# A quarter of the gate weights loaded early, on few partitions, in a decode kernel that streams a KV cache

## The chip, the cores and the metric

The kernel runs on one core of one Trainium2 chip. The metric is the device time of one execution in microseconds (us); the median of three runs before is 663.46 us.

## The reference, cut to what matters

```python
mod = (_silu(c) @ w_mod).reshape(c.shape[0], 6, 1, -1)     # c: 4 x 512, w_mod: 512 x 3072
sa, ca, ga, sb, cb, gb = (mod[:, 0].copy(), ..., mod[:, 5].copy())
h = _layernorm(x, axis=-1) * (1 + ca) + sa
x = x + ga * _A_ref(h, A_k_cache, A_v_cache, A_wq, A_wo)   # 4 tokens, 32 heads, 4096 cached keys, 128 per head
h = _layernorm(x, axis=-1) * (1 + cb) + sb
x = x + gb * _B_ref(h, B_w_in, B_w_sp, B_b_sp, B_w_out)    # gated MLP, 512 -> 1792 -> 512
return x
```

Everything is bf16. Attention reads two caches of 4 x 32 x 4096 x 128, 128 MiB each. The six sections of `w_mod` (512 columns each) make shifts, scales and gates; the last section gives `gb`, which multiplies the MLP's result just before the output. So `gb` is needed at the very end, though it depends on `c` and `w_mod` alone.

## The kernel before, in words

The kernel streams K and V once through three big buffers in SBUF: bA and bB hold K (64 KB on each of 128 partitions), bC holds V. Work goes in 32 rounds `i`, each for four heads of one batch; two rounds share a load of 8 MB (`load_k`, `load_v`, both issued on SP's queue at L145). In a round, DVE multiplies K by the query in two halves (`mult`, L376), PE adds up most of the products with identity matmuls (`reduce_d`, L384) and DVE the rest (L396, L407). After every second round DVE finds the maximum, ACT takes the exponentials into the tile pbd (L450), and PE multiplies them with V (`pv`, L505). A V load may start when `pv` has read the V before it; a K load when DVE has summed the K before it. The order is written out by hand in the loop over `i`, with no scheduler; each engine runs its instructions in the order in which the program names them.

Before the rounds, bC holds wq in its first 32 KB per partition, five of the six sections of w_mod behind it (`wm_sb`, one transfer, L127), and small tiles (`pre`). PE multiplies silu(c), laid out as columns in cT, with these sections (`mod_rows`, L272): the results stand as rows in `mrows` and are turned into columns by transposes (`mod_turn`, L282). Two sections are needed for the queries (L321, L329). The other three go through `late_mod_b`, called in round 0 between DVE's second multiplication and its first sum, which copies them into modT (L352). As soon as PE has read what lies in bC, the first V load replaces it.

At the end the last V load comes in four cuts (`TAIL`, 64, 32, 16 and 16 columns of 128), and bC is filled by `load_end`: the last part of wo in two transfers, w_in in two, w_out in two, and the gate section of w_mod in four (L596, `KG`), one for each quarter of its 512 rows, 128 partitions by 1 KB. The MLP's two products are `gate` (L825) and the one into `y` (L851); then comes the product of the gate section with cT (L859, 16 matmuls of 4 columns), DVE's chain that joins y, the layer norm's numbers and gb (L879 to L891), a transpose (L893), the residual (L895) and the output (L896).

A transfer adds to one of eight semaphores, which are given out in turn, four of ACT's transfers included. Before a transfer is issued, the eighth before it must have landed. In the kernel before there are 52 transfers on SP's queue and four on ACT's (c, x, and two single elements).

`ps_sm` gives out three small PSUM buffers in turn. `across` is an f32 product of a 128 x 128 matrix with a narrow tile (L216).

Of the kernel before, what the change touches and what calls it, by code (L numbers as in the profile page):

```python
# [8 lines left out]
BF16 = mybir.dt.bfloat16  # L9
F32 = mybir.dt.float32  # L10
# [6 lines left out]
HP = 8  # L17
# [1 line left out]
RD = 8  # L19
TAIL = (64, 32, 16, 16)  # L20
KIN = (slice(0, 2), slice(2, 4))
KG = tuple(slice(k, k + 1) for k in range(4))
JW = (slice(0, 4), slice(4, 7))
RW = (slice(0, 4), slice(4, 8))

# [26 lines left out]
def kernel(  # L52
# [16 lines left out]
    nc = tc.nc  # L69
    P = 128  # L70
    B, _, D = A_x.shape
# [3 lines left out]
    DJ = D // P  # L75
# [4 lines left out]
    R = P // HQ  # L80
    G = 4
    NT = B * H // HQ
    GP = H // HP - 1
# [12 lines left out]
    ident_bf = front.tile([P, P], BF16, name="ident_bf")  # L96
# [3 lines left out]
    bufA, bufB, bufC = bufs  # L100
    consts = ctx.enter_context(tc.tile_pool(name="consts", bufs=1))
    wk = ctx.enter_context(tc.tile_pool(name="work", bufs=2))
    psum = ctx.enter_context(tc.tile_pool(name="psum", bufs=1, space=PSUM))
    KB = 1024
# [4 lines left out]
    def ps_sm(shape, dtype=F32):  # L109
        return psum.tile(shape, dtype, name="sm", bufs=3)  # L110

    def ps_q():
        return psum.tile([P, 512], F32, name="qps", bufs=1)

    wq_sb = Arena(bufC, 0, 32 * KB).tile([P, DJ, H * DH], BF16)
    wm_sb = Arena(bufC, 32 * KB, 52 * KB).tile([P, DJ, 5 * D], BF16)
    pre = Arena(bufC, 52 * KB, 64 * KB)
    cx_sb = pre.tile([2 * B, D], BF16, name="cx_sb")
# [5 lines left out]
    nc.scalar.preload_act_table_set("natural_log_exp_and_others")  # L124
    nc.sync.dma_start(out=wq_sb, in_=A_wq.rearrange("(p j) n -> p j n", p=P))
    wm = w_mod.rearrange("(p j) n -> p j n", p=P)
    nc.sync.dma_start(out=wm_sb, in_=wm[:, :, 0:5 * D])  # L127

    def kv_view(cache, i):
        if i < N0:  # L130
# [17 lines left out]
    def load_k(i):  # L148
        if i < N0:
            load(bufs[i // 2 % 2], kv_view(A_k_cache, i), (NJ, NJ) if i == 0 else (NP,))  # L150
        else:
            load(kts[i], kv_view(A_k_cache, i), (NJ,))
# [5 lines left out]
            load(vts[i], kv_view(A_v_cache, i), TAIL if i == L else (NJ,))  # L158

    load_k(0)  # L160
    load_k(2)

    make_identity(nc, ident_bf)
    ident_f = consts.tile([P, P], F32, name="ident_f")
# [16 lines left out]
    def spread(n, pattern, axis, **sizes):  # L181
# [18 lines left out]
        out=far, in0=half, scalar1=-1.0, scalar2=-NEG, op0=ALU.add, op1=ALU.mult  # L200
    )
    nc.gpsimd.tensor_scalar(
        out=fars, in0=far[:, :, None].to_broadcast([P, 2, R // 2]), scalar1=-1.0, scalar2=None, op0=ALU.mult
    )
    cT = consts.tile([P, DJ, B], BF16, name="cT")
    pbd8 = consts.tile([P, NP, HP], BF16, name="pbd")
    nc.gpsimd.memset(pbd8, 0.0)
    pbds = pbd8.rearrange("p n q -> p (n q)").rearrange("p (k n q) -> p k n q", k=4, q=HQ)
# [42 lines left out]
    for j in range(DJ):  # L251
        nc.tensor.transpose(cxp[:, j, :], cx_sb[:, j:D:DJ], ident_bf[0:2 * B, 0:2 * B])
    cps, xps = cxp[:, :, 0:B], cxp[:, :, B:2 * B]
    cx = pre.tile([P, DJ, B], F32, name="cx")
    nc.vector.tensor_copy(out=cx, in_=cps)
    sg = pre.tile([P, DJ, B], F32, name="sg")
    nc.vector.tensor_scalar(
        out=sg, in0=cx, scalar1=-60.0, scalar2=-1.0, op0=ALU.max, op1=ALU.mult
    )
# [5 lines left out]
    mrows = pre.tile([P, D], F32, name="mrows")  # L265
# [13 lines left out]
    def mod_turn(n):  # L279
        mps = ps_sm([P, DJ, n * R])  # L280
        for j in range(DJ):
            nc.tensor.transpose(mps[:, j, :], mrows[0:n * R, j:D:DJ], ident_f[0:n * R, 0:n * R])  # L282
        return mps.rearrange("p j (s r) -> p s j r", s=n)[:, :, :, 0:B]
# [10 lines left out]
        out=hs, in0=modA[:, 1], scalar=1.0, in1=xn, op0=ALU.add, op1=ALU.mult  # L294
# [19 lines left out]
    def queries(n):  # L314
        h, b = divmod(n, B)
        gs = slice(h * GQ, (h + 1) * GQ)
        if b == 0:
            qr = ps_sm([P, GQ, DH])
            for k in range(DJ):
                for q in range(HQ):  # L320
                    nc.tensor.matmul(  # L321
                        qr[R * q:R * (q + 1)], lhsT=hT[:, k, :], rhs=wq_v[:, k, gs, q, :],
                        start=(k == 0), stop=(k == DJ - 1), tile_position=(0, R * q),
                    )
            nc.scalar.copy(out=qrow[:, h], in_=qr)
        qp = ps_q().rearrange("p (g d) -> p g d", g=GQ)
        npair = 1 if h and b == BL else 2
        for k in range(2):
            nc.tensor.matmul(  # L329
                qp[:, 0:npair], lhsT=eb2[k][:, b].rearrange("p k q r -> p (k q r)"),  # L330
                rhs=qrow[:, h, k:2 * npair:2], start=(k == 0), stop=(k == 1),
            )
        if npair == 1:
            nc.tensor.matmul(
                qp[:, 2:4], lhsT=eb[:, b].rearrange("p q r -> p (q r)"), rhs=qrow[:, h, 2:4],
                start=True, stop=True,
            )
            nc.scalar.copy(out=qbo, in_=qp[:, 2:4])
        nc.scalar.copy(out=qbp[:, 2 * h:2 * h + npair, b, :], in_=qp[:, 0:npair])  # L339

    for n in range(2 * B):
        queries(n)

    modT = consts.tile([P, 3 * DJ, B], F32, name="modT")
    g8 = consts.tile([P, 2, B], F32, name="g8")
    spf = consts.tile([P, 2], F32, name="spf")

    def late_mod_b():
        mps = mod_turn(3)
        sps = ps_sm([P, 2])  # L350
        nc.tensor.matmul(sps, lhsT=ones_b, rhs=sp_t, start=True, stop=True)
        nc.vector.tensor_copy(  # L352
            out=modT.rearrange("p (s j) b -> p s j b", s=3),
            in_=mps,
        )
        nc.vector.tensor_copy(out=spf, in_=sps)
        nc.gpsimd.tensor_copy(out=g8[:, 1, :], in_=spf[:, 0:1].to_broadcast([P, B]))
        cbT = modT[:, 2 * DJ:3 * DJ, :]
        nc.gpsimd.tensor_scalar_add(out=cbT, in0=cbT, scalar1=1.0)
# [208 lines left out]
    wo_sb = Arena(bufA, 0, 24 * KB).tile([P, GP * HP, D], BF16)  # L568
# [1 line left out]
    wol_sb = Arena(bufC, 0, 8 * KB).tile([P, HP, D], BF16)  # L570
    win_sb = Arena(bufC, 8 * KB, 22 * KB).tile([P, DJ, F], BF16)
    wout_sb = Arena(bufC, 22 * KB, 29 * KB).tile([P, NH, D], BF16)
    wg_sb = Arena(bufC, 29 * KB, 33 * KB).tile([P, DJ, D], BF16)
    tl = Arena(bufC, 33 * KB, 64 * KB)
    NL = GP * HP * DH

    def load_wo():
        nc.sync.dma_start(
            out=wo_sb.rearrange("p (k r) n -> p k r n", r=HP),
            in_=A_wo[0:NL].rearrange("(k p r) n -> p k r n", k=GP, p=P),  # L580
        )

    def load_end():
        wol = A_wo[NL:H * DH].rearrange("(p r) n -> p r n", p=P)
        for rs in RW:
            nc.sync.dma_start(out=wol_sb[:, rs], in_=wol[:, rs])
        win = B_w_in.rearrange("(p j) n -> p j n", p=P)
        for ks in KIN:
            nc.sync.dma_start(out=win_sb[:, ks], in_=win[:, ks])
        for js in JW:  # L590
            nc.sync.dma_start(
                out=wout_sb[:, js],
                in_=B_w_out[js.start * P:js.stop * P].rearrange("(p j) n -> p j n", p=P),
            )
        for ks in KG:
            nc.sync.dma_start(out=wg_sb[:, ks], in_=wm[:, ks, 5 * D:])  # L596

    acc = late.tile([P, DJ, B], F32, name="acc")
    st2 = late.tile([P, 2, B, DJ + 1], F32, name="st2")
# [73 lines left out]
    for i in range(NT):  # L673
        mult(i, 0)
        if i >= 1:
            scores(i - 1)
        for k in normed_in(i - 1):
            norm_b(k)
        pick = i - 3 if i % 2 == 0 and i >= 4 else None
        if i % 2 and 3 <= i < L:  # L680
            pv(i - 2)
        if i % 2 and i < N0:
            load_v(i)
        reduce_d(i, 0)
        if pick:
            o_pick(pick)
            o_cols(pick)
        if i == L:
            deal(2)
            pv(N0 - 1)  # L690
            load_end()
            nc.gpsimd.memset(pbd8, 0.0)  # L692
            nc.vector.memset(opss[1], 0.0)
            exps(N0)
        mult(i, 1)
        if i == 0:
            late_mod_b()
        for k in normed_in(i):
            norm_r(k)
        if pick:  # L700
            o_scale(pick)
        sum8(i, 0)
        if i == L:
            dealt(0, 0, 2 * B)
            dealt(2)
            o_pick(N0 - 1)
            nc.vector.memset(opss[0], 0.0)
        reduce_d(i, 1)
        sum_rest(i)
        for k in normed_in(i):  # L710
            norm_a(k)
        if i == L - 1:
            deal(0, 0, 2 * B)
        if i == L:
            o_cols(N0 - 1)
            project()
        if i % 2 and i + 3 < N0:
            load_k(i + 3)
        elif i == N0 - 3:
            load_k(N0)  # L720
            load_k(L)
        elif i == N0 - 1:
            load_wo()
            load_v(N0)
            late_consts()
        elif i == N0:
            load_v(L)
# [16 lines left out]
    for i in (N0, L):  # L744
        norm_a(i)
    nc.vector.tensor_reduce(
        out=sel32, in_=ident_f.rearrange("p (q r) -> p r q", r=R), axis=AX.X, op=ALU.add
# [69 lines left out]
    def gate(h, part):  # L817
# [26 lines left out]
        out=zz.rearrange("p f g b -> p g b f"), in0=z1[:, None].to_broadcast([P, 2, B, NH]),  # L844
        in1=st3[:, 0:2], op=ALU.mult,
    )
    y = ps_q()[:, 0:DJ * 2 * B].rearrange("p (j g b) -> p j g b", j=DJ, g=2)
    for js in JW:
        for j in range(DJ):
# [3 lines left out]
                    start=(j == 0 and f == 0), stop=(f == NH - 1), skip_group_check=True,  # L853
                )

    gb = ps_sm([P, DJ, B])
    for k in range(DJ):
        for j in range(DJ):
            nc.tensor.matmul(  # L859
                gb[:, j, :], lhsT=wg_sb[:, k, j * P:(j + 1) * P], rhs=cT[:, k, :],  # L860
                start=(k == 0 and j == 0), stop=(k == DJ - 1), skip_group_check=True,
            )
    mq3 = tl.tile([P, 2, B], F32, name="mq3")
    nc.vector.tensor_reduce(
# [62 lines left out]
```

## Time and profile before

| | |
|---|---|
| Median of 3 runs | 663.46 us (663.36 to 663.65) |
| Profiled execution: time, span | 663.69 us, 661.8 us |
| Moved by DMA | 283.07 MB, mean 428 GB/s |
| Queue of SP | 8016 packets, 282.73 MB, 99.0% of 16 engines' span |
| Busy: DVE, PE, ACT | 574.8, 309.7, 171.9 us |
| Largest waits of SP's queue | V landings 279.0 us, DVE's sums L396 180.1 us, PE's L505 86.1 us |
| Chain that ended last | DMA 64%, DVE 16%, PE 14%, ACT 4% |

The span runs from the first instruction to the last; 1.9 us of the execution's time lie outside it. Idle time of an engine that is not the bottleneck costs nothing. SP's queue is not an engine that moves data: it only issues transfers, and waits in it matter when the DMA engines run out of packets. Times in the text are from the span's start.

### The profile page before, as it was taken

To read this page: it belongs to the slowest core of one execution; us is meant where nothing else is said; L and a number is where in the kernel's file an instruction comes from. 1 tells how busy PE (TensorE), PEld (TensorE's weight loads), DVE (VectorE), ACT (ScalarE), POOL (GpSimd) and SP (SyncE) were. 2 spreads that over 40 slices of the span, in tenths; PEclk is the share of its full clock that TensorE was granted. 3 is DMA by queue.
4 is the path that set the end of the run, shared out by engine and by line. 5 is a ranking of instruction groups with operands and counts; after the bars stand their busy time and mean duration, and the time that the engine had idled before them with its cause. 6 is when DMAs were issued, how large, how long until landed. Compare 5 with 4: busy or idle time off the path is not lost.

```text
span 661.8 us, 5002 instructions
## 1 busy us (share of the span) xinstructions
PE 309.7 (47%) x2036; PEld 130.4 (20%) x2036; DVE 574.8 (87%) x367; ACT 171.9 (26%) x284; POOL 19.0 (3%) x56
## 2 busy tenths in 40 slices
PE   0554454536253463615336361534635245463885
PEld 0121121212021121202112120211212012121434
DVE  2269999999898998989899898979979898999943
ACT  1220414223060603206060330605023060503322
POOL 3000000000000000000000000000000000040100
PEclk9996686867677785767777576777756778675975
DMA  8999999999999999999999999999999999999997
GB/s 364 450 423 444 444 437 440 444 400 437 436 444 433 440 417 432 445 424 440 437 440 420 440 433 424 436 445 444 413 444 429 432 440 433 428 420 449 412 419 283
DMA packets 8060, 283.07 MB, mean 428 GB/s; under 512 B 860, under 2 KB 1380, under 8 KB 2916
## 3 DMA queue, kind: packets, MB, share of 16 engines
q1 hardware_dynamic: 8016, 282.73, 99.0%
q8 instruction: 16, 0.26, 0.1%
q14 instruction: 8, 0.07, 0.0%
q10 hardware_dynamic: 20, 0.01, 0.0%
HBM read 282.73 MB, written 0.00 MB: 427 GB/s over the span
## 4 chain that ended last, share of the span: by engine, by line
DMA 64%; DVE 16%; PE 14%; ACT 4%; issue 1%; SPq 0%; POOL 0%; ACTq 0%; DVEq 0%
DMA bC<-in_A_v_cache_dram 50%; PE ops L505 9%; DVE S L396 6%; DMA bA<-in_A_k_cache_dram 6%; DVE bA L376 4%; DMA bC<-in_A_wo_dram 4%; DMA bC<-in_w_mod_dram 4%; DVE bB L376 3%; ACT pbd L450 3%; PE red L384 3%; DVE S L407 1%; PE qps L329 1%; PE sm L321 1%; PE sm L272 1%; ACT qbp L339 0%
## 5 line engine op out<-in xcount | busy, mean ns | idle before, releaser
L450 ACT ACTIVATE pbd<-S,nb 32x256 bf16<-32x256 f32 x120 | 154.2, 1519 | 423.1 <-DVE nb L437 421.9
L376 DVE TENSOR_TENSOR bA<-bA,qbp 128x8192 bf16<-128x8192 bf16 x32 | 142.7, 4462 | 21.1 <-DMA bA<-in_A_k_cache_dram 21.1
L384 PE MATMUL red<-bB,ident_bf 128*128 128x512 bf16 x344 | 97.2, 441 | 116.2 <-DVE bB L376 116.0
L384 PE MATMUL red<-bA,ident_bf 128*128 128x512 bf16 x320 | 91.8, 446 | 121.0 <-DVE bA L376 121.0
L384 PEld LDWEIGHTS <-ident_bf 128*128 128x128 bf16 x664 | 72.0, 110 | 350.7 <-issue 195.0
L376 DVE TENSOR_TENSOR bB<-bB,qbp 128x8192 bf16<-128x8192 bf16 x28 | 123.7, 4417 | 14.1 <-DMA bB<-in_A_k_cache_dram 14.1
L505 PE MATMUL ops<-bC,pbd 128*32 128x512 bf16 x960 | 80.1, 507 | 67.3 <-DMA bC<-in_A_v_cache_dram 58.5
L396 DVE TENSOR_REDUCE S<-bA 128x48 f32<-128x6144 bf16 x16 | 104.7, 6542 | 0.0
L396 DVE TENSOR_REDUCE S<-bB 128x48 f32<-128x6144 bf16 x14 | 91.6, 6542 | 0.0
L505 PEld LDWEIGHTS <-pbd 128*32 128x32 bf16 (+1 forms) x1016 | 36.0, 122 | 117.4 <-issue 59.1
L450 ACT ACTIVATION_READ_ACCUMULATOR pbd<-S,nb 32x1 f32 x120 | 58.7, 489 | 0.0
L407 DVE TENSOR_REDUCE S<-red 128x64 f32<-128x512 f32 x64 | 43.7, 682 | 2.7 <-PE red L384 2.5
L464 POOL TENSOR_TENSOR rsb<-maskd,rs 128x8 f32<-128x8 f32 x15 | 3.1, 204 | 562.0 <-ACT pbd L450 562.0
L376 DVE TENSOR_TENSOR bB<-bB,qbo 128x8192 bf16<-128x8192 bf16 x4 | 17.6, 4411 | 0.0
L517 DVE TENSOR_REDUCE osb<-ops 128x128 f32<-128x512 f32 x17 | 11.8, 692 | 0.6
L514 DVE TENSOR_TENSOR ops<-ops,m 128x512 f32<-128x512 f32 x15 | 10.4, 693 | 0.0
L483 PE MATMUL sm<-rsb,inv_d 128*128 128x32 f32 (+2 forms) x12 | 2.9, 338 | 13.9 <-POOL rsb L464 13.9
L293 DVE SCALAR_TENSOR_TENSOR bC<-sm,bC 128x16 f32<-128x16 f32 x1 | 0.2, 175 | 10.1 <-PE sm L282 10.1
L450 ACT ACTIVATE pbd<-S,nM 32x128 bf16<-32x128 f32 x8 | 4.6, 576 | 11.6 <-POOL pbd L692 10.1
L420 DVE TENSOR_REDUCE mrow<-S 128x1 f32<-128x256 f32 (+1 forms) x17 | 6.9, 404 | 0.6
L272 PE MATMUL sm<-bC,cT 128*4 128x512 bf16 x20 | 3.7, 621 | 7.1 <-DMA bC<-in_w_mod_dram 7.1
L329 PE MATMUL qps<-bC 128*128 128x256 bf16 (+1 forms) x16 | 4.5, 382 | 4.1 <-ACT qbp L339 2.8
(159 smaller groups left out, 128.1 us busy)
## 6 DMA issues: line engine op xcount, KB each, us to landing
bA<-in_A_k_cache_dram SPq DMA_DIRECT2D x2, 4096.0 KB, 31.3
bB<-in_A_k_cache_dram SPq DMA_DIRECT2D x2, 4096.0 KB, 41.1
bC<-in_A_wq_dram SPq DMA_DIRECT2D x1, 4096.0 KB, 12.3
bA<-in_A_v_cache_dram SPq DMA_DIRECT2D x1, 4096.0 KB
bA<-in_A_wo_dram SPq DMA_DIRECT2D x1, 3072.0 KB, 39.9
bC<-in_w_mod_dram SPq DMA_DIRECT2D x1, 2560.0 KB, 17.9
bB<-in_A_v_cache_dram SPq DMA_DIRECT2D x1, 2048.0 KB, 31.9
bC<-in_B_w_in_dram SPq DMA_DIRECT2D x2, 896.0 KB, 24.1
```

What stands on the lines that cost most here:

```text
L272: nc.tensor.matmul(mp[R * s:R * s + B], lhsT=cT[:, k, :], rhs=wm_sb[:, k, (s0 + s) * D:(s0 + s + 1) * D], start=(k == 0), stop=(k == DJ - ...
L321: nc.tensor.matmul(qr[R * q:R * (q + 1)], lhsT=hT[:, k, :], rhs=wq_v[:, k, gs, q, :], start=(k == 0), stop=(k == DJ - 1), tile_position=(0 ...
L329: nc.tensor.matmul(qp[:, 0:npair], lhsT=eb2[k][:, b].rearrange("p k q r -> p (k q r)"), rhs=qrow[:, h, k:2 * npair:2], start=(k == 0), sto ...
L376: nc.vector.tensor_tensor(out=kt, in0=kt, in1=bc(q, KC), op=ALU.mult)
L384: nc.tensor.matmul(red, lhsT=ident_bf, rhs=kt[:, :, m * rd:(m + 1) * rd], start=(m == 0), stop=(m == DH // rd - 1),)
L396: nc.vector.tensor_reduce(out=st[i, "S"][:, n0:NJ], in_=kts[i][:, n0:NJ, :], axis=AX.X, op=ALU.add)
L407: nc.vector.tensor_reduce(out=st[i, "S"][:, kc * KC:kc * KC + on_pe(i, kc)], in_=st.pop((i, "red", kc)), axis=AX.X, op=ALU.add,)
L420: nc.vector.tensor_reduce(out=mrow, in_=S, axis=AX.X, op=ALU.max)
L450: nc.scalar.activation(out=pbd8[r, :, 2 * q + h] if pair(i) else pbds[r, i % 4, :, q], in_=S[r, :], func=AF.Exp, bias=nM[r, h:h + 1], scal ...
L505: nc.tensor.matmul(ops_of(i)[g:g + rows], lhsT=pb[:, n, :], rhs=vt[:, n, :], start=(m < 4), stop=(m >= end - 4), tile_position=(0, g),)
L514: nc.vector.tensor_tensor(out=ops, in0=ops, in1=sel[:, :, None].to_broadcast([P, G, DH]), op=ALU.mult)
L517: nc.vector.tensor_reduce(out=osb, in_=ops.rearrange("p g d -> p d g"), axis=AX.X, op=ALU.add)
```

## The change

128 of the 512 rows of the gate section go into bC early, in place of wq, and are multiplied with silu(c) in round 0. The result is a fourth group of rows in `mrows`, turned together with the other three, and kept in modT. The remaining 384 rows are loaded at the end as before, three to a partition.

- The 128 rows: 120 as 12 partitions of 10 rows, by four transfers of three partitions each (0, 4, 8; then 1, 5, 9; and so on), and 8 rows as 8 partitions of one row. All five are issued behind the queries, where wq has been read, and ahead of the third K load, `load_k(2)`, which was issued at the start before.
- cT gets columns for these row layouts, by 14 more transposes and three more copies. The rest of silu works on all columns at once.
- `mod_uneven`: 11 matmuls on 12 (or 8) partitions and an ACT copy, ahead of `late_mod_b`.
- At the end the early part of gb, still f32 in modT, is added by a product with the identity, which starts the accumulation into gb ahead of y; 12 matmuls of the other rows follow y.
- w_mod's five sections come in three transfers (one, one and two rows a partition) in place of one, the first part of wo in three in place of one. SP's queue then has 60 transfers, with ACT's 64.

```diff
-KG = tuple(slice(k, k + 1) for k in range(4))
+KE = 3
+KG = tuple(slice(k, k + 1) for k in range(KE))
+EV = 128 * KE
+PU = 12
+RU = 10
+EU = EV + PU * RU
+MR = (slice(0, 1), slice(1, 2), slice(2, 4))
...
-    nc.sync.dma_start(out=wm_sb, in_=wm[:, :, 0:5 * D])
+    for ks in MR:
+        nc.sync.dma_start(out=wm_sb[:, ks], in_=wm[:, ks, 0:5 * D])
...
     load_k(0)
-    load_k(2)
+    wgu_sb = Arena(bufC, 0, (RU + 1) * KB).tile([P, RU + 1, D], BF16)
...
+    cuts = [(P, slice(k, EV, KE)) for k in range(KE)]
+    cuts += [(PU, slice(EV + r, EU, RU)) for r in range(RU)] + [(D - EU, slice(EU, D))]
+    cup = ps_sm([P, len(cuts), B], BF16)
+    for n, (pn, cut) in enumerate(cuts):
+        nc.tensor.transpose(cup[0:pn, n, :], cx_sb[0:B, cut], ident_bf[0:B, 0:B])
...
     for n in range(2 * B):
         queries(n)
-
-    modT = consts.tile([P, 3 * DJ, B], F32, name="modT")
+    wu = w_mod[EV:EU, 5 * D:].rearrange("(p r) n -> p r n", r=RU)
+    for b in range(4):
+        nc.sync.dma_start(out=wgu_sb[b:PU:4, 0:RU], in_=wu[b:PU:4])
+    nc.sync.dma_start(out=wgu_sb[0:D - EU, RU], in_=w_mod[EU:D, 5 * D:])
+    load_k(2)
+
+    modT = consts.tile([P, 4 * DJ, B], F32, name="modT")
...
+    def mod_uneven():
+        mp = ps_sm([P, D])
+        for r in range(RU + 1):
+            pn = PU if r < RU else D - EU
+            nc.tensor.matmul(
+                mp[3 * R:3 * R + B], lhsT=cT[0:pn, DJ + KE + r, :], rhs=wgu_sb[0:pn, r, :],
+                start=(r == 0), stop=(r == RU), tile_position=(0, 3 * R),
+            )
+        nc.scalar.copy(
+            out=mrows[3 * R:3 * R + B].rearrange("b (p j) -> b j p", j=DJ),
+            in_=mp[3 * R:3 * R + B].rearrange("b (j p) -> b j p", j=DJ),
+        )
...
-        mps = mod_turn(3)
+        mps = mod_turn(4)
...
     def load_wo():
-        nc.sync.dma_start(
-            out=wo_sb.rearrange("p (k r) n -> p k r n", r=HP),
-            in_=A_wo[0:NL].rearrange("(k p r) n -> p k r n", k=GP, p=P),
-        )
+        wo = A_wo[0:NL].rearrange("(k p r) n -> p k r n", k=GP, p=P)
+        for k in range(GP):
+            nc.sync.dma_start(out=wo_sb.rearrange("p (k r) n -> p k r n", r=HP)[:, k], in_=wo[:, k])
...
+        wge = w_mod[0:EV, 5 * D:].rearrange("(p k) n -> p k n", p=P)
         for ks in KG:
-            nc.sync.dma_start(out=wg_sb[:, ks], in_=wm[:, ks, 5 * D:])
+            nc.sync.dma_start(out=wg_sb[:, ks], in_=wge[:, ks])
...
         if i == 0:
+            mod_uneven()
             late_mod_b()
...
+    gb = ps_sm([P, DJ, B])
+    nc.tensor.matmul(
+        gb.rearrange("p j b -> p (j b)"), lhsT=ident_f, rhs=modT[:, 3 * DJ:4 * DJ, :].rearrange("p j b -> p (j b)"),
+        start=True, stop=False, skip_group_check=True,
+    )
...
-    gb = ps_sm([P, DJ, B])
-    for k in range(DJ):
+    for k in range(KE):
         for j in range(DJ):
             nc.tensor.matmul(
-                gb[:, j, :], lhsT=wg_sb[:, k, j * P:(j + 1) * P], rhs=cT[:, k, :],
-                start=(k == 0 and j == 0), stop=(k == DJ - 1), skip_group_check=True,
+                gb[:, j, :], lhsT=wg_sb[:, k, j * P:(j + 1) * P], rhs=cT[:, DJ + k, :],
+                start=False, stop=(k == KE - 1), skip_group_check=True,
             )
```

More of the change, by code (lines that the diff above doesn't have):

```diff
@@ L204 @@
     )
-    cT = consts.tile([P, DJ, B], BF16, name="cT")
+    NC = DJ + KE + RU + 1
+    cT = consts.tile([P, NC, B], BF16, name="cT")
     pbd8 = consts.tile([P, NP, HP], BF16, name="pbd")
@@ L253 @@
     cps, xps = cxp[:, :, 0:B], cxp[:, :, B:2 * B]
-    cx = pre.tile([P, DJ, B], F32, name="cx")
-    nc.vector.tensor_copy(out=cx, in_=cps)
-    sg = pre.tile([P, DJ, B], F32, name="sg")
+    cuts = [(P, slice(k, EV, KE)) for k in range(KE)]
[3 more added lines that the diff above has]
+        nc.tensor.transpose(cup[0:pn, n, :], cx_sb[0:B, cut], ident_bf[0:B, 0:B])
+    cx = pre.tile([P, NC, B], F32, name="cx")
+    nc.gpsimd.memset(cx[:, DJ + KE:], 0.0)
+    nc.vector.tensor_copy(out=cx[:, 0:DJ], in_=cps)
+    nc.vector.tensor_copy(out=cx[:, DJ:DJ + KE], in_=cup[:, 0:KE])
+    nc.vector.tensor_copy(out=cx[0:PU, DJ + KE:NC - 1], in_=cup[0:PU, KE:KE + RU])
+    nc.vector.tensor_copy(out=cx[0:D - EU, NC - 1], in_=cup[0:D - EU, KE + RU])
+    sg = pre.tile([P, NC, B], F32, name="sg")
     nc.vector.tensor_scalar(
@@ L352, in late_mod_b @@
         nc.vector.tensor_copy(
-            out=modT.rearrange("p (s j) b -> p s j b", s=3),
+            out=modT.rearrange("p (s j) b -> p s j b", s=4),
             in_=mps,
@@ L572 @@
     wout_sb = Arena(bufC, 22 * KB, 29 * KB).tile([P, NH, D], BF16)
-    wg_sb = Arena(bufC, 29 * KB, 33 * KB).tile([P, DJ, D], BF16)
+    wg_sb = Arena(bufC, 29 * KB, 33 * KB).tile([P, KE, D], BF16)
     tl = Arena(bufC, 33 * KB, 64 * KB)
```

## The prediction

> **What bounds the kernel now.** I read the page's slices and queues first, then the waits, then the chain that ended last, and last the timeline from 618 us on. The slices say which resource is full:
>
> ```profile
> DMA  8999999999999999999999999999999999999997
> ...
> q1 hardware_dynamic: 8016, 282.73, 99.0%
> q8 instruction: 16, 0.26, 0.1%
> q14 instruction: 8, 0.07, 0.0%
> ```
>
> The DMA engines are busy for 99% of the span with the transfers of SP's queue, while DVE has 87% and PE 47%. So a time here is an engine's list of packets. The trace keeps start, length, size and queue of each packet, though not its engine; as a packet starts some 4 ns before the one ahead ends, I could follow sixteen chains. A 64 KB packet takes 2.418 us on every one, and an 8 MB transfer 19.32 us. What sets engines apart is the last two rows above: the sixteen 16 KB instruction packets take about 0.93 us each and the data packet behind them 2.9 us instead of 2.418, so 1.4 us; the eight of 8 KB take 0.31 us, and with the packet behind them 0.55 to 0.84 us. None is won back. When the first V half of the last four rounds has landed (about 635 us), the chains stand, behind the foremost, at some 0.0 to 0.1 us (five), 0.50, 0.93, 1.42, 1.47, 2.40, 2.55, 2.76, 2.80, 2.84, 2.99 and 3.00 us. A landing is the slowest chain's.
>
> That matters at the end, where PE has caught up and waits for each cut of V:
>
> ```profile
> 643.02 1.65 PE L505 MATMUL ops<-bB,pbd 128*16 128x512 bf16 x16 [0.67 <-DMA bB<-in_A_v_cache_dram]
> ...
> 645.47 0.61 PE L505 MATMUL ops<-bB,pbd 128*16 128x512 bf16 x8 [0.49 <-DMA bB<-in_A_v_cache_dram]
> ...
> 646.69 0.56 PE L539 MATMUL qps<-pbd,bB 128*128 128x4 bf16 x16 [0.61 <-DMA bB<-in_A_v_cache_dram]
> ```
>
> The column in brackets is the idle time and what ended it. From 645.47 on a fixed chain of computing runs to the end, whose last part is:
>
> ```profile
> 656.00 0.68 PE L216 MATMUL sm<-bA 128*128 128x56 f32 x2
> ...
> 656.18 0.41 DVE L843 TENSOR_TENSOR bC<-bC,bA 128x56 bf16<-128x56 f32 x1 [0.24 <-ACT bC L838]
> ...
> 656.64 0.89 PE L851 MATMUL qps<-bC 128*128 128x8 bf16 x28
> ...
> 657.56 0.19 DVE L879 TENSOR_TENSOR bC<-g,qps 128x32 f32<-128x32 f32 x1 [0.17 <-PE qps L851]
> ...
> 658.01 0.51 PEld L859 LDWEIGHTS <-bC 128*128 128x128 bf16 x8 [0.23 <-DMA bC<-in_w_mod_dram]
> ...
> 658.27 0.17 DVE L890 TENSOR_TENSOR bC<-bC 128x16 f32<-128x16 f32 x1
> ...
> 658.65 0.17 DVE L891 TENSOR_TENSOR bC<-bC,sm 128x16 f32<-128x16 f32 x1 [0.20 <-PE sm L859]
> ```
>
> The gate's last quarter is what L891 waits for, but by only 0.2 us: its other input is ready at 658.27 + 0.17 = 658.44. So two lists end together here, the slowest engine's packets and the computing from the V cuts on.
>
> **The change, part by part.** *Gate rows leave the end.* One of four gate transfers goes. On a chain it is 8 packets of 1 KB at 42.4 ns and a 9 ns semaphore packet: 0.35 us. The last landing, 657.96 in the packets, comes to 657.61 on the slow chains. L891 can use 0.18 us of that (658.65 to 658.44 and a hand-over of 0.03).
>
> *Gate rows come in early.* Four transfers of three partitions by ten 1 KB rows, and one of eight rows. The nearest row for their placing is ACT's queue: c and x, four partitions each, left 4 data and 4 semaphore packets each, on four chains and no others. So I put 40 packets on each of three chains: 4 x (10 x 42.4 + 9) = 1.73 us, with the eight rows' packet 1.79 us. The other thirteen take 0.05 us at most. By the gate transfer saved, the three chains are 1.44 us worse at the end, but the full 1.79 us worse when the V cuts land. The Trainium skill (DMA: Bandwidth & Descriptors, Why a DMA increments its semaphore by 16 and not by 1) says that such a transfer runs on the largest number up to 16 that divides the slowest dimension, on the lowest-numbered engines; its Rules for kernel authors warn against outermost dimensions under 16 for that reason. By that page the sum is the same 1.79 us on engines 0 to 2, and the four chains agree.
>
> Whether it costs depends on the three chains' lags. Of the four that carried c and x, the one that also carried the two one-element loads is the first. Another is certain: it took 8 KB instruction packets at 103, 343 and 632 us, and is the one at 2.55 us. The remaining two I lose between 100 and 200 us, where ends of several chains come within 1 ns; they are among chains that stand at 0.0 to 0.1, 0.93, 1.4 to 1.5 or 2.8 us. Three of the four get the new rows, the first always, so the chain at 2.55 us is among them in two cases of three. It then stands at 2.55 + 1.79 = 4.34 us, 1.34 us behind what is now the slowest (3.00). If it is spared and no other late one is hit, nothing of the 1.79 us shows, as 0.93 + 1.79 is below 3.0.
>
> The Trainium skill (Runtime: NRT & Kernel Launch, Instruction fetch mechanics) calls the cost of crossing a 16 KiB block mostly hidden. By it the chains would be level and the change would cost all of 1.79 us; the 1.4 us per packet above says otherwise.
>
> *SP's queue.* The third K load (L145, `load_k(2)`) now stands behind a wait for the last wq product (L321, over at 31.84) and five more issues; at 0.40 us each (L125) its issue ends at 34.3 us. The queue has the first K loads to work on until 37.7 us, so this is hidden by 3.4 us. w_mod's three pieces and wo's three add two semaphore packets each: 4 x 9 ns = 0.04 us on all chains. SP's later waits for the eighth transfer before shift to pieces of wo, which land at 628 us at the latest; what is issued behind them is needed from 640 us on.
>
> *Early computing.* Fourteen transposes and three DVE copies fit before 19.1 us, where PE waits 7.1 us for w_mod. `mod_uneven` puts 11 matmuls of 512 columns on PE at the rate of L643 (24 in 5.34 us): 2.4 us, and an ACT copy like L277 (0.59). DVE's copy L352 waits 3.1 us longer, and all of DVE's work behind it, up to the third and fourth K halves. The V load behind it moves from 43.3 to 46.5 us and is needed at 57; the next K load moves from 68.5 to 71.7 and is needed at 76.3; DVE's own 4.25 us of idle time at 98.2 us takes the rest. No cost; without that cover it would be 3.1 us.
>
> *The early product's way out.* `gb` is started by an f32 product with the identity, on PE between L216 and L851. f32 products of 16 columns take 0.61 us there (L216 at 639 us, two passes with their weight loads). Bounds: zero, were it hidden behind DVE's zz, which ends at 656.59, and 0.61 us. It can't be hidden whole, as L216 holds PE until 656.64; one weight load of 0.25 us can overlap, and I take 0.46 us. L851 and the DVE chain behind it move by that: L891's other input comes at 658.90. Four of sixteen products of L859 fall away, off the path.
>
> **Sum, forecast.** V cuts 1.34 + 0.04 later; the end's 0.46 more for the identity product, less 0.18 as the gate no longer ends last: +1.66 us. On the profiled execution (span 661.8, its time 663.69, so 1.9 us around it) that is 665.35; on the median of 663.46, which lies 0.23 lower, 665.1 us. With the identity hidden or whole it is +1.2 to +1.8 us; if a chain at 2.84 us is hit, 2.84 + 1.79 - 3.00 = 1.63 in place of 1.34, so up to +2.1 us.
>
> **Rivals.** *The three chains are ahead (not slower).* The chain at 2.55 us is the fourth of the four, and the others have 0.1 to 0.93 us. For it: five to six chains are at the front, and 1.79 us fits in their 3.0. Against: one known late chain among three places. V cuts move by 0.04 us only; -0.18 + 0.46 + 0.04 = +0.3 us, 663.8 us, and 663.3 with the identity hidden. It decides as soon as no chain over 1.21 us (3.00 - 1.79) gets the rows.
>
> *The third K load comes too late.* Were the wait to reach to the last query (36.24 us), its issue would end at 38.7 and its packets start 0.65 us later (as for wq), against 37.7: thirteen engines idle for 1.6 us, and all later landings with them. With +0.3 that is 665.4 us. Against it: the new rows lie where wq lay, in the first 11 KB of bC, and L321 is the last to read there. It decides where the issue is over 3.4 us later than I work out.
>
> *Three partitions do not use three engines.* If all go on one, it gets 120 packets, 5.2 us; with 0.1 us of lag and 3.0 of slack +2.3, in all 665.8 to 666.1. If they were spread on all, the change would be worth what its end is, +0.3 us. The four packets of c on four chains speak against both.
>
> **How the numbers follow.** A late chain is hit: 0.52. The three are ahead: 0.37. A late K load or one engine: 0.06. Something faster that I see no row for: 0.05, since nothing before the V cuts gets shorter on the slow chains. 0.2% is 1.33 us, about what a measurement of this kernel can tell from no change. Of the first case 0.06 lies below it (identity hidden), so slower is 0.46 + 0.06 = 0.52, same 0.06 + 0.37 = 0.43, faster 0.05. The range goes from the second case's lower bound, 663.3, to the first's upper part, 665.8; the forecast's own is 664.7 to 665.6.
>
> **What would show it.** Right: the waits of L505 and L539 for V's cuts (numbers of their lines shifted) end 1.4 us later, DMA busy as now; a gate landing that no longer ends the wait of the last product; L851 starting about 0.46 us later behind the end of L216. Wrong: V cuts at the same time within 0.1 us means the three chains were ahead; a dent in GB/s in the third slice means the K load; DVE starting its sum of round 0 more than 8 us later would put the next K load late.

## The result and the profile after

| | before | after |
|---|---|---|
| Median, first comparison (12 runs each) | 663.67 us (663.36 to 664.04) | 665.27 us (664.12 to 666.25) |
| Ratio, 95% interval | | 1.0023 [1.0014, 1.0032] |
| Profiled execution: time, span | 663.69, 661.8 us | 664.16, 662.4 us |

The change makes the kernel 1.6 us slower. The number of the forecast, 665.1 us, is met; the reason that it gave is not the one that the traces show. The changed kernel also spreads over 2.1 us where the kernel before spreads over 0.7, and the profiled execution of it is one of its fastest. Line numbers after the change are higher: L145 is L152, L216 L224, L352 L387, L505 L540, L539 L574, L851 L892, L859 L899, L891 L931.

The page after the change has the same picture of a DMA bound, with the same instruction packets:

```profile
DMA  8999999999999999999999999999999999999996
...
q1 hardware_dynamic: 8084, 282.73, 99.0%
q8 instruction: 16, 0.26, 0.1%
q14 instruction: 8, 0.07, 0.0%
```

The timeline, PE's waits for the last cuts of V after the change (start, length, instruction, and in brackets the idle time and what ended it):

```profile
643.27 1.04 PE L540 MATMUL ops<-bB,pbd 128*16 128x512 bf16 x16 [1.05 <-DMA bB<-in_A_v_cache_dram]
...
645.70 0.99 PE L540 MATMUL ops<-bB,pbd 128*16 128x512 bf16 x8 [1.07 <-DMA bB<-in_A_v_cache_dram]
646.93 0.59 PE L574 MATMUL qps<-pbd,bB 128*128 128x4 bf16 x16 [0.25 <-DMA bB<-in_A_v_cache_dram]
```

In this execution the cuts come 0.2 us later than before (645.70 against 645.47, 646.93 against 646.69), not 1.4. By the prediction's own list that says that the three engines were ahead. The end, in the same timeline:

```profile
656.45 0.68 PE L224 MATMUL sm<-bA 128*128 128x56 f32 x2
...
656.91 0.57 PE L884 MATMUL sm<-modT,ident_f 128*128 128x16 f32 x2
...
657.32 0.89 PE L892 MATMUL qps<-bC 128*128 128x8 bf16 x28
...
658.04 0.53 PEld L899 LDWEIGHTS <-bC 128*128 128x128 bf16 x12
...
659.23 0.17 DVE L931 TENSOR_TENSOR bC<-bC,sm 128x16 f32<-128x16 f32 x1
```

L899's weight load no longer waits for the gate transfer, and L931 no longer waits for L899: the gate is off the path. The identity product L884 stands between L224 and L892, whose distance grows from 0.64 us (656.00 to 656.64) to 0.87. So 0.58 us at L931 are 0.23 of later cuts, 0.22 of the computing between (below), 0.23 of the identity product, and -0.10 for the gate.

The 0.22 us between go with the granted clock after the last cut. By stretches (busy time of PE, PEld, DVE, ACT and POOL, then PEclk, DMA share and GB/s), before and after:

```profile
645.00:647.00 2.00, 0.92 (x20) 0.42 (x20) 1.00 (x3) 0.00 (x0) 0.00 (x0) 1.00 1.03 421
```

```profile
645.00:647.00 2.00, 1.06 (x10) 0.17 (x10) 0.27 (x1) 0.00 (x0) 0.00 (x0) 0.70 1.03 420
```

The clock falls to half inside this stretch after the change (at 645.78 us; before, at 647.71), and the eight products at 645.70 take 0.99 us where they took 0.61. That is one execution against another.

What differs early is one line. SP issues the second V load of the rounds (V3: bC, for rounds 2 and 3) 3.56 us later. Timeline of SP from 84 to 101 us, before and then after:

```profile
90.25 0.33 SPq L145 DMA_DIRECT2D bC<-in_A_v_cache_dram  x1
```

```profile
93.81 0.33 SPq L152 DMA_DIRECT2D bC<-in_A_v_cache_dram  x1
```

The load ahead of it (K4, the K of rounds 4 and 5) ends on the first engine at 95.63 us before and at 95.70 after. Before, V3's first packets take the usual 2.42 us. After, 14 packets of 64 KB that start between 94.4 and 98.6 us take 2.5 to 4.3 us, 0.37 us per engine too long on the mean (one of the 14 stands behind an instruction packet, as one does before). The foremost engine, 0.07 us behind at 95.7, starts its first 16 KB packet of V at 634.98 instead of 634.63. And V3 is late because DVE is, in round 0, though not by that alone. DVE's copy into modT among the groups by line (idle time ahead of it and what ended it in the last column), before and after:

```profile
L352 DVE COPY modT<-sm 128x48 f32<-128x48 f32 x1 | 0.2, 208 | 5.5 <-PE sm L282 5.5
```

```profile
L387 DVE COPY modT<-sm 128x64 f32<-128x64 f32 x1 | 0.2, 224 | 8.3 <-PE sm L299 8.3
```

V3's issue waits for PE's products with the V load before it. Their first row in the timeline, before and after:

```profile
85.28 4.92 PE L505 MATMUL ops<-bC,pbd 128*32 128x512 bf16 x64 [5.05 <-ACT pbd L450]
```

```profile
87.53 6.23 PE L540 MATMUL ops<-bC,pbd 128*32 128x512 bf16 x64 [5.06 <-ACT pbd L485]
```

They start 2.25 us later, and the same 64 products take 1.31 us longer: the granted clock was at half from 84.51 to 87.92 us before and from 86.00 to 92.82 us after. So of V3's 3.56 us, 2.25 are DVE's delay and 1.31 the clock.

### The profile page after: what moved, and what is told of

It is laid out like the page before. It is cut to its first block, busy times and chain, and to the rows that moved or that the text cites. A ratio compares the mean times of both kernels' runs of the same rounds, so it can differ in the third digit from the quotient of the medians.

```text
span 662.4 us, 5067 instructions
## 1 busy us (share of the span) xinstructions
PE 315.0 (48%) x2059; PEld 132.2 (20%) x2059; DVE 575.6 (87%) x370; ACT 173.2 (26%) x285; POOL 18.8 (3%) x57
## 4 chain that ended last, share of the span: by engine, by line
DMA 54%; DVE 29%; PE 13%; ACT 3%; issue 1%; SPq 0%; ACTq 0%; DVEq 0%
DMA bC<-in_A_v_cache_dram 35%; DMA bA<-in_A_k_cache_dram 13%; DVE S L431 11%; DVE bA L411 9%; PE ops L540 7%; DVE bB L411 5%; DMA bB<-in_A_v_cache_dram 5%; DMA bC<-in_w_mod_dram 3%; PE red L419 3%; DVE S L442 2%; ACT pbd L485 2%; PE qps L346 1%; PE sm L338 1%; DVE osb L552 1%; DVE ops L549 0%
## 5 line engine op out<-in xcount | busy, mean ns | idle before, releaser
L419 PE MATMUL red<-bB,ident_bf 128*128 128x512 bf16 x344 | 93.3, 427 | 118.7 <-DVE bB L411 118.7
L540 PE MATMUL ops<-bC,pbd 128*32 128x512 bf16 x960 | 85.6, 535 | 67.3 <-DMA bC<-in_A_v_cache_dram 54.6
L540 PEld LDWEIGHTS <-pbd 128*32 128x32 bf16 (+1 forms) x1016 | 37.2, 128 | 122.8 <-issue 67.4
L387 DVE COPY modT<-sm 128x64 f32<-128x64 f32 x1 | 0.2, 224 | 8.3 <-PE sm L299 8.3
```

The costliest lines, as they stand in the source:

```text
L419: nc.tensor.matmul(red, lhsT=ident_bf, rhs=kt[:, :, m * rd:(m + 1) * rd], start=(m == 0), stop=(m == DH // rd - 1),)
L540: nc.tensor.matmul(ops_of(i)[g:g + rows], lhsT=pb[:, n, :], rhs=vt[:, n, :], start=(m < 4), stop=(m >= end - 4), tile_position=(0, g),)
```

## The experiments

Four theories. U is the forecast: 1.79 us of extra packets put a late engine further back. I is the identity product, S the 3 us of DVE by themselves. D is the one that the trace after suggested: V3 is issued so late that the DMA engines nearly run out of work at 95.7 us, and lose time there. Each ratio is against the kernel before on the same chip, with its 95% interval.

**The rows on twelve engines (e1).**

```diff
-    for b in range(4):
-        nc.sync.dma_start(out=wgu_sb[b:PU:4, 0:RU], in_=wu[b:PU:4])
+    nc.sync.dma_start(out=wgu_sb[0:PU, 0:RU], in_=wu)
```

> The changed kernel, but its 120 early gate rows come in one transfer of 12 partitions in place of four of three, so twelve DMA engines get 10 packets each (0.43 us) and none 40 (1.73 us). Theory U (the extra packets make three engines late, and with them the V cuts): the median falls from 665.3 by 1.0 to 1.5 us, to about 664.0. Theory I (the early product's way out and other computing at the end cost the time, the extra packets fit in what the three engines are ahead): within 0.3 us of 665.3.

Measured: 665.29 us, 1.0024 [1.0015, 1.0033]. No better; but this doesn't refute U by itself. The first packets of K2 (the third K load) behind the 120 small ones took 2.8 to 3.8 us, in the median 3.44, instead of 2.42, 0.94 us per engine too long, which put the whole stream back, so that K4 ended at 96.94 and V3 (again at 93.81) came 3.1 us ahead of that: no long packets at V3. One loss took the place of another. Why K2's first packets are long here, and not behind the transfers of three partitions, stays open; K2 was issued at 31.32 us, 6.4 us ahead of the end of the load before it, so that a late issue is not the reason.

**The identity product ahead of the gate products (e2).**

```diff
+    gb = ps_sm([P, DJ, B])
+    nc.tensor.matmul(gb..., lhsT=ident_f, rhs=modT[:, 3 * DJ:4 * DJ, :]..., start=True, stop=False, ...)
     gate(1, 0)
```

> The changed kernel, but the product with the identity that starts gb stands on PE ahead of the MLP's first products, where PE waits, instead of between L224 and L892. Theory I: L892 starts about 0.25 to 0.5 us after L224 earlier than in the changed kernel, and the median falls by 0.2 to 0.6 us, or by 1.3 us if that product costs all of the loss. Theory U: the same 0.2 to 0.5 us at most, with more than 1 us of the loss left.

Measured: 665.06 us, 1.0019 [1.001, 1.0029]. L224 to L892 is 0.64 us again (657.57 to 658.21), so the 0.23 us go; the rest stays. In this execution V3 went out at 95.31 us; the engines stood idle for 0.50 us on the mean ahead of it, and the long packets cost 0.56 us per engine.

**Only the pieces of w_mod and wo (e3), and only the rows (e4), in the kernel before.**

```diff
-    nc.sync.dma_start(out=wm_sb, in_=wm[:, :, 0:5 * D])
+    for ks in (slice(0, 1), slice(1, 2), slice(2, 4)):
+        nc.sync.dma_start(out=wm_sb[:, ks], in_=wm[:, ks, 0:5 * D])
...
+        for k in range(GP):
+            nc.sync.dma_start(out=wo_sb.rearrange("p (k r) n -> p k r n", r=HP)[:, k], in_=wo[:, k])
```

> The kernel before, with w_mod's five sections in three transfers and wo's first part in three, and nothing else of the change: 60 transfers. Theory U and theory I: 663.7, as before, within 0.2 us (four semaphore packets of 9 ns on each engine). Theory S (the pieces cost the time, through the waits for the eighth transfer before): 664.5 to 665.3.

```diff
-    load_k(2)
...
+    for b in range(4):
+        nc.sync.dma_start(out=wgu_sb[b:12:4, 0:10], in_=wu[b:12:4])
+    nc.sync.dma_start(out=wgu_sb[0:8, 10], in_=w_mod[504:D, 5 * D:])
+    load_k(2)
```

> The kernel before, with the five early loads added (four of three partitions, one of eight) and the third K load behind them, but nothing computed from them: the gate section is loaded whole at the end, so these 128 KB are moved twice. Theory U: V cuts and the end 1.0 to 1.5 us later, 664.7 to 665.2. Theory I: 663.7 to 664.0.

Measured: the pieces 664.08 us, 1.0005 [0.9996, 1.0014]; the rows, unused, 663.95 us, 1.0004 [0.9995, 1.0013]. Both intervals hold 1. The rows cost 0.24 us (at most 0.9 by the interval) where U says 1.4: U falls as the explanation of the 1.6 us.

**DVE's sums first (e5).** The two calls move behind the sums of round 0; everything else of the change stays.

```diff
         if i == 0:
-            mod_uneven()
-            late_mod_b()
...
         sum_rest(i)
+        if i == 0:
+            mod_uneven()
+            late_mod_b()
```

> The changed kernel with one thing moved: mod_uneven and late_mod_b are called after the sums of round 0 instead of ahead of them, so VectorE no longer waits for them (it waited 8.35 us ahead of L387's copy in the changed kernel, 5.48 us ahead of L352's in the kernel before). Everything else of the change stays. Theory D (the delay of VectorE in round 0 makes the second V load be issued too late: 93.81 us instead of 90.25, where the last packets of the load ahead of it end at about 95.6, and the DMA engines lose about 0.4 to 0.6 us there, each): V3 is issued before 90.3 us, no long packets at 95 us, median 664.1 to 664.5 (what is left are the pieces, the rows and the identity product, 0.3 to 0.8 us). Theory U (the 1.79 us of extra packets on three engines, the forecast): stays at 665.1 to 665.4, whenever V3 is issued. Theory S (the 3.1 us on VectorE act later, in some other place than V3): V3's issue may change, but the foremost engine's first V-cut packet stays at 634.98.

Measured: 663.96 us (663.80 to 664.39), 1.0007 [0.9998, 1.0015]. DVE does not wait, V3 goes out early, and the spread is that of the kernel before again. Groups by line and timeline of SP:

```profile
L387 DVE COPY modT<-sm 128x64 f32<-128x64 f32 x1 | 0.2, 216 | 0.0
```

```profile
87.90 0.33 SPq L152 DMA_DIRECT2D bC<-in_A_v_cache_dram  x1
```

So two calls' place is worth 1.2 of the 1.6 us, with all extra packets still there.

**The delay alone (e6), doubled (e7), halved (e9).** The kernel before, with 11, 25 or 5 dead products and a dead copy ahead of the late modulation. No load differs.

```diff
+    def dead_rows():
+        mp = ps_sm([P, D])
+        for r in range(11):
+            nc.tensor.matmul(mp[3 * R:3 * R + B], lhsT=cT[0:12, r % DJ, :], rhs=wm_sb[0:12, r % DJ, 0:D], ...)
+        nc.scalar.copy(out=mrows[3 * R:3 * R + B]..., in_=mp[3 * R:3 * R + B]...)
...
-        mps = mod_turn(3)
+        mps = mod_turn(4)[:, 0:3]
...
+            dead_rows()
             late_mod_b()
```

> The kernel before with the delay alone: eleven dead products (0.23 us each) and one dead ACT copy with the strided pattern of the changed kernel stand ahead of late_mod_b, which turns four groups of rows instead of three; no load is added, moved or split. Theory D: VectorE waits 8.3 us instead of 5.5 in round 0, V3 is issued at 93.5 to 94 us instead of 90.25, the packets at about 96 us are 0.3 to 0.6 us longer on each engine, and the median is 664.1 to 664.7, with runs further apart than the 0.8 us of the kernel before. Theory U (extra packets): no load differs, so 663.6 to 663.9. Theory I (the identity product) and the pieces: 663.7 as well.

> As the delay alone, but with 25 dead products: VectorE waits about 11.5 us instead of 5.5. Theory D: V3 is issued at about 97 us, after the load ahead of it has ended at 95.6, so the DMA engines stand idle for about 3 us (issue to the first packets is some 2 us): median 666 to 668. If the delay acted in proportion, and not from a threshold, it would be twice the effect of the delay alone. Theories U and I: 663.7 to 663.9, as no load is added.

> As the delay alone, but with five dead products instead of eleven. From the two earlier runs (eleven: V3 issued 4.1 us later than in the kernel before, +1.95 us; 25: 8.4 us later, +5.5 us) one product is 0.31 us of V3's issue, so V3 goes out at about 92.2 us. Theory D with a threshold (the line through the two runs meets zero at an issue of about 92 us): 663.6 to 664.0, no long packets at 96 us. Loss in proportion to the delay from zero on: 664.5. If the loss has no threshold but comes from VectorE being late anywhere, 664.5 as well.

Measured: the delay alone 665.60 us, 1.0028 [1.0019, 1.0036], with runs from 664.30 to 666.26; doubled 669.07 us, 1.0083 [1.0069, 1.0097]; halved 663.75 us, 1.0004 [0.9995, 1.0013]. The delay alone makes the whole loss of the change. It exceeds what theory D had expected (664.1 to 664.7), and so does the doubled one, where 666 to 668 was expected. SP's timeline of the three, in this order:

```profile
94.36 0.33 SPq L145 DMA_DIRECT2D bC<-in_A_v_cache_dram  x1
```

```profile
75.94 0.33 SPq L145 DMA_DIRECT2D bA<-in_A_k_cache_dram  x1
98.68 0.33 SPq L145 DMA_DIRECT2D bC<-in_A_v_cache_dram  x1
```

```profile
92.14 0.33 SPq L145 DMA_DIRECT2D bC<-in_A_v_cache_dram  x1
```

Half the delay is free, the full one is not, and the doubled one hits twice: K4 too is issued only 0.4 us before the load ahead of it ends, and its first packets come 0.5 us after that end and 0.63 us per engine too long; at V3 the engines stand idle for 2.7 us on the mean (the last ends at 97.34, the first packet starts at 99.64) and lose 0.68 us more. That makes 4.5 us, as late as the foremost engine starts its first 16 KB packet of V (639.14 instead of 634.63). The expectation had put some 2 us between an issue and its first packets; here it is 0.96 us from the start of V3's issue. The page of the doubled delay shows V3's part in GB/s, in the sixth and seventh of 40 slices (83 to 117 us): 363 and 394, where the kernel before has 437 and 440. The rows of the doubled delay and of the kernel before:

```profile
GB/s 364 453 448 405 441 363 394 441 434 441 441 430 429 409 442 441 438 429 437 438 437 434 433 421 441 438 425 429 438 437 438 437 441 418 441 416 447 413 419 279
```

```profile
GB/s 364 450 423 444 444 437 440 444 400 437 436 444 433 440 417 432 445 424 440 437 440 420 440 433 424 436 445 444 413 444 429 432 440 433 428 420 449 412 419 283
```

**The kernel before with its sums first (e10).**

```diff
-        if i == 0:
-            late_mod_b()
...
         sum_rest(i)
+        if i == 0:
+            late_mod_b()
```

> The kernel before with late_mod_b called after the sums of round 0, and nothing else: VectorE does not wait 5.48 us for L351's product, and V3 is issued 2 to 4 us earlier than 90.25. Theory D with a threshold: no gain, 663.4 to 663.8, as the load ahead of V3 ends no sooner. Loss in proportion to VectorE's wait: 1 us or more faster, 662 to 662.7.

Measured: 663.52 us, 1.0000 [0.9991, 1.0009]; V3 at 89.10 us. Nothing is won by being earlier than early enough: a threshold.

**All remedies (e8).** The move of e5, the identity product as in e2, and w_mod and wo in one transfer each as before.

> The changed kernel with the three remedies together: the early computing after the sums of round 0, the identity product ahead of the gate products, and w_mod's first load and w_o's in one transfer each again. What stays of the change is the five early loads of 128 rows and the shorter gate transfer. Theory D with the small terms as the earlier runs gave them (pieces 0.37, rows 0.24, identity product 0.2): 663.7 plus the rows' 0.24 minus up to 0.35 for the shorter gate transfer, so 663.5 to 663.9: within 0.2 us of the kernel before. Theory U: 664.9 to 665.2, as the extra packets are still there.

Measured: 664.07 us, 1.0007 [0.9998, 1.0016]. It is not separable from e5, and above the 663.5 to 663.9 that D and the small terms gave. No version is faster than the kernel before; e10 equals it.

**Three engines far behind (e11).** The rows alone, of 3 KB instead of 1 KB.

```diff
-    load_k(2)
+    wgu_sb = Arena(bufC, 0, 30 * KB).tile([P, 10, 3 * D], BF16)
...
+    wu = w_mod[384:504, 3 * D:].rearrange("(p r) n -> p r n", r=10)
+    for b in range(4):
+        nc.sync.dma_start(out=wgu_sb[b:12:4, 0:10], in_=wu[b:12:4])
+    nc.sync.dma_start(out=wgu_sb[64:72, 0], in_=w_mod[504:D, 3 * D:])
+    load_k(2)
```

> The kernel before with five dead early loads of 128 rows ahead of K2, as the rows alone, but each row is 3 KB (0.121 us a packet in this kernel's trace) instead of 1 KB (0.046): three engines carry 40 packets or 4.7 us more than the others. In the changed kernel the three stood 1.64, 1.69 and 2.72 us behind the foremost with 1.79 us of extra packets, and the last of the others 3.10; with 4.7 us they stand 4.5 to 5.6 behind. Theory U as to its price (engines keep what they are behind until the V cuts; only what goes beyond the last of the others counts): V cuts 1.5 to 2.5 us later, median 665.2 to 666.3, with V3 issued at 90.3 as before. If extra packets on few engines never come through to the end: 663.6 to 664.1.

Measured: 667.58 us, 1.0059 [1.0047, 1.0072], more than expected. In its packets three engines stand 4.95, 5.34 and 6.98 us behind the foremost at the V cuts, all others within 3.32; the 3 KB packets took 0.13 us on the mean instead of 0.121. Against the slowest before, 3.15 us, that is 3.8 us more, and 0.2 us of the foremost: 4.0, as the time says. The 0.2 us go with a late refill again: K2 was issued at 35.79 us, 1.9 us ahead of the end of the load before it, and 13 of its first packets took 2.5 to 3.3 us, 0.26 us per engine too long. In e4 it was issued 3.4 us ahead, and none of them was long. V3 went out at 92.37 us, later than expected, but 3.8 us ahead, with no long packet but one behind an instruction packet. PE's waits:

```profile
642.33 1.03 PE L510 MATMUL ops<-bA,pbd 128*16 128x512 bf16 x8 [2.95 <-DMA bA<-in_A_v_cache_dram]
...
647.19 0.93 PE L510 MATMUL ops<-bB,pbd 128*16 128x512 bf16 x8 [0.63 <-DMA bB<-in_A_v_cache_dram]
```

So the price model of U is right: an engine's packets are never won back, and beyond the last of the others they cost what they are. At 1.79 us they were under it.

**The changed kernel again (e12).** The same file, for a second trace.

> The changed kernel once more, for a second trace beside the one that took 664.16 us, 1.1 us under its median. Theory D: V3 is issued at 93.5 to 95.5 us again and about 15 packets of 64 KB that start between 94.5 and 97.5 us are long; if this execution is nearer to the median, the excess is larger than the 0.35 us per engine of the first trace, or one engine keeps a lead less of 1 to 2 us from it up to the V cuts. Median 664.9 to 665.6. Theory U with another assignment of the chains: the slowest V cuts come from an engine with 41 early packets, 1 us or more behind the last of the others.

Measured: 665.18 us (664.13 to 666.55), 1.0028 [1.0019, 1.0037]; this trace is of an execution of 666.11 us. V3 is issued at 94.26 us and 13 packets are long. The last V cut's last packet ends at 647.48, not 645.24 as in the first trace, because one engine stands 5.03 us behind the foremost, where the slowest before has 3.15:

```profile
645.43 1.45 PE L540 MATMUL ops<-bB,pbd 128*16 128x512 bf16 x16 [0.62 <-DMA bB<-in_A_v_cache_dram]
647.88 0.61 PE L540 MATMUL ops<-bB,pbd 128*16 128x512 bf16 x8 [0.69 <-DMA bB<-in_A_v_cache_dram]
```

Its ends of loads show how: at 231.7 us the last engine is 2.19 us behind, at 251.0 it is 3.61, at the end 5.03, twice 1.42 for the PE instruction packets at 238.7 and 592.7. Before, the packet at 238.6 met an engine 0.16 us behind. In the trace of the delay alone it is the same (2.07, 3.49, 4.91). After a late refill the engines stand in another order, and in some executions the one that takes these two packets is among the last. In e12 it is the engine that lost most at V3: its first packet starts at 96.83 us, 0.8 to 1.0 us after its part of the load ahead ended, and takes 4.18 us. In the delay alone its first packet starts at 97.43 us, at least 1.4 us after its part of the load ahead ended. In the first trace the longest packet (4.32 us) fell on another engine. That fits the wider spread; what decides which engine loses most stays open.

V3's lead in eight traces (from its issue to the first engine's end of the load ahead; the median of before is that of the first comparison, those of the later ones are 663.5 to 663.7):

| kernel | median us | V3 issued | load ahead ends | lead | 64 KB packets over 2.45 us, 94.4 to 98.6 us |
|---|---|---|---|---|---|
| before | 663.67 | 90.25 | 95.63 | 5.4 | 1 |
| e10, sums first | 663.52 | 89.10 | 95.59 | 6.5 | 1 |
| e9, half delay | 663.75 | 92.14 | 95.69 | 3.6 | 1 |
| e1, twelve engines | 665.29 | 93.81 | 96.94 | 3.1 | 1 |
| after | 665.27 | 93.81 | 95.70 | 1.9 | 14 |
| e12, after again | 665.18 | 94.26 | 95.64 | 1.4 | 13 |
| e6, delay alone | 665.60 | 94.36 | 95.65 | 1.3 | 13 |
| e2, identity early | 665.06 | 95.31 | 95.59 | 0.3 | 14 |

The single long packet is one behind an instruction packet. At V3 a lead of 3.1 us or more is enough, one of 1.9 is not. Why packets behind a late issue are long stays open.

## Why the prediction was right, and where not

**What bounds the kernel** held. In all traces the time is the end of the last V cut's last packet plus 18.5 to 19.0 us: before 645.10 and 663.69, after 645.24 and 664.16, e12 647.48 and 666.11, e6 647.10 and 665.60, e11 649.15 and 667.91.

**Which engines.** The transfers did use three engines, with 40 small packets each and 1.79 us, as worked out from the four chains of c and x. The chain at 2.55 us was taken to be among them in two cases of three. It was spared: in the trace after, the engine with 8 KB instruction packets at 103.6, 343.5 and 625.2 us has one early packet, not 41. In the V load that the foremost engine ends at 588.6 us the three stand 1.64, 1.69 and 2.72 us behind it, the last of the others 3.12. So the forecast's term of 1.34 us did not occur, and its first rival described the engines; e4 and e5 show it (0.24 and 0.36 us), e11 that the rule behind the term holds once the slack is used up. The prediction's list of what each engine is behind counts from a point 0.15 us behind the foremost engine, so that its 3.00 us is the 3.15 us here; the differences between the engines are not touched by that.

**Early computing, "no cost": the step that failed.** It took DVE's 3.1 us past three loads and gave the leads of two: the first V load, needed at 57 us, and K4, needed at 76.3. The rest was to go into 4.25 us of DVE's idle time at 98.2 us, and there is none. The chain that ended last has the first line below; the timeline of DVE in the same execution has the second, so that DVE works on until 102.54 us:

```profile
98.20 4.25 issue
```

```profile
96.00 6.54 DVE L396 TENSOR_REDUCE S<-bB 128x48 f32<-128x6144 bf16 x1
```

After the change DVE starts that sum at 98.23 us and is still 2.2 us late behind it; in the kernel before, it next waits for a K load only ahead of 175.23 us (for 1.53 us). V3, ahead of that place, was not looked at. Its lead was 5.4 us and became 1.9, and 1.31 us of that fall go with the granted clock; the next smallest after the change is K4's, 5.6. Even with that figure the step would have called it hidden, since 1.9 us is more than an issue takes to its first packets. That this does not suffice is what no row of the trace before showed. The prediction's own price, "without that cover it would be 3.1 us", was the right place and, with 1.2 us (after against e5) to 2.0 us (the delay alone) measured, too high.

The Trainium skill (DMA: Bandwidth & Descriptors, Specifications) gives about 0.6 us to the first byte on SP's path. In e7, where the engines stood idle, the issue ended at 99.01 and the first packets started at 99.64: they agree. By that figure a lead of 1.9 us would be enough, and the 14 long packets say that it is not.

**The total is right by accident.** The forecast's sum was 1.38 us of late cuts, 0.46 of identity and -0.18 of gate. What stands in their place is 1.2 us of late refill and 0.4 of all else.

**Small terms.** Identity product: 0.23 us in the trace, where 0.46 was taken between 0 and 0.61; L884 starts 0.2 us before L224 ends, and L892's weight loads before L884 ends. Gate: -0.10 instead of -0.18. Third K load: its issue ends at 33.9 us, 34.3 was predicted, with no gap. Pieces: 0.04 us was predicted; 0.37 was measured, with 0 inside the interval. What is left in e5, 0.36 us, has a plausible place that was not tried by itself: as I follow the chains there, the slowest, 0.4 us behind the slowest before, is one with 41 early packets and three 8 KB instruction packets.

**The chances.** The likeliest outcome came, over 0.2% slower, with half the chance, but through a case with no chance of its own. A rival "V3 too late" belonged beside "the third K load too late", which was worked out in detail.

## What to carry to other kernels

When a step delays an engine that frees buffers, list every load whose issue hangs on that engine until the delay is taken up, with the time at which the queue runs out, and look for the smallest lead; one unchecked load decides. In this kernel, bound by DMA, the lead had to cover not only the time from issue to first packet but a good deal more, at V3 over 1.9 us and at most 3.1. Whether a step of the chain called "issue" is idle time is read from the engine's own timeline. Side work for the end of a kernel should stand behind, not ahead of, the instructions that free the next buffer: moving two calls by a few lines gave back 1.2 of 1.6 us.

## What the runs showed of the hardware

A refill that comes just in time is not free: with 0.3 to 1.9 us of lead the first 64 KB packet of most engines takes 2.5 to 4.3 us instead of 2.42, and the engines leave it in another order. Some also stand idle ahead of it: all of them for 0.50 us on the mean at 0.3 us of lead (e2), single ones for about 1 us or more at 1.3 and 1.4 us (e6, e12). With a negative lead (e7, V3) the idle time and long packets of 2.68 to 3.47 us add up. Of two executions of the same program with the same long packets, one can then be 2 us slower than the other, since it depends on which engine later takes two instruction packets that cost 1.42 us each. The granted clock moved V3 too: the same 64 products took 4.92 us before and 6.23 us after.
